# Four more idle transposes at the start of a fused threshold-attention and max-of-three feed-forward kernel, with a new written order

## The chip, the cores and the metric

The kernel runs on one core of one Trainium2 chip, in one launch. The metric is the device time of that launch in microseconds; smaller is better. The engines are called PE (matrix multiply; its weight loads are PEld), DVE (vector), ACT (scalar), POOL (GpSimd) and SP (the queue that issues most DMAs).

## The reference

Eight batches, eight heads, 576 positions of 64 dimensions. An attention keeps, in each row of scores, only the entries within tau = 0.02 of the row's maximum; its output, heads put side by side, is the input of a feed-forward step that takes the largest of three products.

```python
scores = scale * np.matmul(q, k.transpose(0, 1, 3, 2))
thresh = np.max(scores, axis=-1, keepdims=True) - tau
scores = np.where(scores >= thresh, scores, -1000000000.0)
scores = scores - np.max(scores, axis=-1, keepdims=True)
attn = np.exp(scores)
attn = attn / (np.sum(attn, axis=-1, keepdims=True) + 1e-09)
out = np.matmul(attn, v)
...
h = np.maximum(np.maximum(x @ w1, x @ w2), x @ w3)
return (h @ w_out).astype(np.float32)
```

q, k, v and the weights are float32; x is 4608 x 512, each of w1, w2, w3 is 512 x 768 and w_out 768 x 512.

## The kernel before

The heads of a batch are worked in two groups of four, called quads. For each quad and each half r (two heads), q and k are loaded (`load`), turned by PE with the help of an identity matrix into a PSUM bank (`transposed`, letter T) and copied out by ACT or DVE (letters a, A for q, c, C for k); POOL makes a second copy of q with its halves exchanged (`swapped`, q). Scores come in half tiles of 128 rows by 576 columns (`scores`, letter S): 288 of them, numbered in the order of the table TILES. One half tile is two pairs of float32 matmuls and fills one of four PSUM banks; the digit behind the letter S, T or F names the bank, and a bank can be filled again when its last reader is done.

A half tile then passes through DVE's maximum (m), ACT's exponent or threshold pass (e), and a second pass that makes the numerators and their sum (n on ACT, or k, a compare-multiply, on DVE). Which way it goes is a digit in the table MASKED: 1 and 3 take the second pass on DVE, 0 and 2 on ACT; 2 and 3 let ACT read the scores from PSUM, so that the bank is held until ACT has passed over it, while with 0 and 1 DVE's maximum frees it. A threshold (th) is made by DVE (s) or POOL (d). A reciprocal (r, DVE) and the normalization (p, POOL) follow, then a DMA that transposes the normalized tile P into ptq (t, on SP). The product of P and v (O, and its second half D, PE) is copied to xt by ACT (x) or DVE (w).

The feed-forward step of a batch begins when its xt is complete: F and B are the two halves of one unit on PE (`ph`, or `po` for the last product), h, H, v copy or combine the results, u, U copy the output to ob, o stores it. The first and the last batch are split in two parts, so that their feed-forward work can begin earlier.

Nothing is scheduled by a program at run time. The string ORDER is the written order: its letters are issued one after the other, each puts its instructions at the end of its engine's queue, and `_Ordered` ties each engine to that order. Capital letters among the copies choose DVE or ACT as said above. Each engine goes through its own queue in that order and waits where its operands or its bank are not ready.

Two groups of PE instructions compute nothing that is used: WARM transposes of the identity matrix at the very start, before the first q lands, and some more ahead of the second half of the first quad's q and k, inside `transposed`.

Of the kernel before, what the change touches and what calls it, by code (L numbers as in the profile page):

```python
# [47 lines left out]
ORDER = """
lllllllllllT2lT0lagqqcT3T2aS1CqqgS3ymgS0emS2ylnmS1emgemT3eS0AeT2kgS3nqmT1CqAnT2rkS1eqmCS0nqmepS2meS3prrmeS1p
tmnS0pS3snkptemeS2prmnzmtemepekpeS3lnS0ylrbyS1nlmtnpmnprremptebS3peS0mpnS1mS2znrmS0eptmnlpS3pemmdlrekS0S1ems  # L50
klT3nAnO20perewdDgpxtmnnT3S0prectpemS2mtS3npreqS0mT1pAptT3S1plqenmbnO02CdrkgmpDlxewzS3emlS0pF2meksBrF3HtS1Bd
S2nntqmetepvelnF0BS1mqS3egvzRnppmnT2nS0pmAdmrpS1peempeS2S1mgknpmegtrtF3BkHS0temS2pmetS1npS3mT2rszneF0mcnnyBs
rS1epsvnO32S0pemDpwsmpewS1nF3S0smrzBrqS1nstmF2vBsT3S0ppemHentnAS1psF2mlT3zyBqrgcvseS3F0nemgS2plpelnmepS3mtyB
ellqrmetqvnpS2sprdmO13fpsS0nDweS1mtewzkmnerS2S0F3dsnpS1mBpmeteepkF0mdtT2BnlulllneRnF1kAstS3pBHnmvF2epyRS0Btm
ppeS1S3vqtnmdS2F0pS1lpmndeT3empBCF2emslnlT3aT1kHdqeBctRvS0yF3S1pptnmnmprdpBF2qS0S1vmenBmltedS3S0HF1epmnrqT2B
mpseanS3veF2T0T1sCapkmBS0etvetyS1rS3ppmmkS0npeetmsO21S3neDxrtpmpnmqS0kS3smpkxS2rmemttpdS1eF0mlpesS3mrS2neBS1
keqnpduT3mlelmpS2O10sklelmCnekRsDwwldS3pteS1pmF2temqS0ntpnpssBeqS3mF1mhF0BBkF2RpS3veseBpvpT0S1ndmepS3HrdnmF2
typamnS0S1esmpnBmrF3vtpesF0S1BBpmvqnrT2enhsS1plS3ecdmnmF0nF2BBnrsptvyS1rveF3etneS0eymF2BS1tmkF0BhBS3ppmqtvlp
veO21edS0rkDmdnlmsnT0eppyxwkeF3loaS2qlT1BnpmesCnRS0HnpmS2seS1mF3mnsS0BeF2ptttpF1pmBBvelqS3lvnhS0snS2F1srrpmm
dF3metpdeBprBvpS2pvnnS0tmosetpS1eerF3ptemT2mAkBpS2UF1nmnnrS0ekqS3eedmmeS2eBptpmuekstlnS3elS0O12rxkmmsrkpDoS3  # L60
pS1rmppemT0oxdeS2N3lpncT1mBqS0nndF2yjtAkqqemT3cnRBdS1edHpF0S3mnepBemS2F1dvBnS3pnemF0tpeS2ntvlmRF1mpyBtdBhkvS
2emedT0F3appT1kttlCpBsS2vF0lpiS1S3mleBmnS2RehtdS1meF0mpnS3dmS2F1pssBtepemmBpnqS3vrnqF2T0dBvnS1mpeApS3rmhmedt
O02knrpleS1dseptnwpDmS0ennwT1lqrF3pmS2BF0pctmrvlqpS1nBemeS3vmdnF2etpeS1BmdtF0pS3BdkrhtmT2vS1ddpS3mekeamnlF0d
pdnRS2nmqF1peBlBepevlHF3nntqS2ppmS0BeF1T2BmvtrCpnS0dvtmS3S2ddpemmtrS1kentF0pS3nT2mBelprmnlpAtT1uS3pcS2eslmqO
01esktemDerwpeS2wS0qnmF1pnmdtnrkS3peS2spmoeBrnmptekS3F0puF2mBertkS1phBssmeS0yF3vnT1mndBllyS2AedyF0edmS1pnBrv
ptF2eS3permBtdpnHF1mlF0pervBdnBdyvetnS3F2HqS1mlnBlpmlS0dF3vpeeT1nlmBlF2kCS0RevBpnS1mpS3hsmpS0eF2smqnBmsnS1pr
veT0plS3maS2tekqO01emddDndmnpweywT3F2lncS0drqmBpF1eeS3yevdT0mBpadlS2HnF3qF0sntrmpBteBqvnsF1tpS2rnvT3pemBS0pt
CrHS2npS3mteF1rmF0dnBeBmyvpeS2lS1lvnpT3lmdeF0ptetsrmpnS2kopS1eBtsmnrmapS2elpS1mnrF3edpmUtS2emqT1neBpkteN0tcu
roS2kBpnS1jmdS3smmpelS0deT1rT2qpmcaS3esmO10nDkS3S2rpexwdmT1nmeanF0rdkleF3BpyS2nteS1sHpBpF0pemmS2rtvsmpqqnBtn
F1evdS3mBhS2repntpmS0mS1F3S2mtnpsrdsBF0S1senBvmdvF3F2etpBnnmqBF1dpHeT0evRBF3cS2vlyedmsBHF0eS1nBeS2tpmnnF3vpp  # L70
S1mrBpenO20tmdF1nvS3wBeskermkS2DelpenhsppqF3mpT1wenyBRS2vdmS0anmnS1mpeF3lS2mpnBqdS0ptF1F2spvimekeBrT3oldhpBv
S0mCeS1tenF3S2lmT0rBpamqS1yS0npS2rnvmmtdpF3eS0ekperBekdtmS1nteteF2pmskS0lmlptmkrBulsesT0ltS3prceS1unnqplmkdO
02lDemS1wqpppRpsS3eeS0mxpmF2lptS1msBS0ntnmS3HmeeymrF1T2dsBF0npS3pnaveesplrpeBtnF2S1BmpnvF0dmHqS3tBlnT2mvksF1
tS3BeCtmF0tF2snvBT3RsBF1eHvS0mepBpeS2atF3dvS0emneBF1nhmnS2nrqesBpO03nmpvwpeS2mnryokpS1DxosT2F0mpS3eecdpF1mtn
BS2qBS3servqphS0T1rmeF2maT3yBmnkS1pvdCmF0S3npBF1edtT2vpettBmF0akS2qheqdBrrsmpnevpS1nntF3pmS2qmBpS0vqmdeS1S2R
nF3T0pmpepCpttmsBS2S0nuF1mmeeksreS3eS0tBemtO32kspnDdrmpywkN3sduweS0onpBsneF1F2nreBjmS0psBnpHpmF3S1tvrpS0pmte
BF2remS1ptBvsF0eS3mBeodnshF2mS1tevBF0F3mBvS2nrF1nnklBmdhBesF2ppvveS0srppS3nreBymF1mS0S3nmemdtBeiphF2F0vdeBBt
vppS3F1nnkeS2mmdehBF0nrrdvnS3epBF2vppF1ntnmrtBthpS0esprsF3BnepeBnmnS2vS0ptpS1vemmmF3dkrS2mBtrS1eeumdO20deDne
O31wS2pDpwepnmnF0xwtkkS1prBS3pemrF1npusF2F0tmeBnpF3drBHpvtBepBnprF1tF2hBF3BvptpF0tvtF1BovhBBO32DvvO01xDxxF2x
uF0F3F2BohF1BF3BBuvovF2F0BoBF1hvvF3BF0hBBvvF2uF0N1BojUoi  # L80
"""


# [728 lines left out]
```

## Time and profile before

| what | value |
|---|---|
| median of the three runs | 443.31 us (441.85 to 444.83) |
| the profiled execution's own time | 444.28 us |
| its span in the trace | 442.5 us |
| mean granted PE clock | 0.983 |
| PE / DVE / ACT / POOL busy | 95% / 88% / 91% / 74% of the span |
| share of the last chain of waits by engine | PE 73%, DVE 7%, ACT 7%, POOL 4%, DMA 3% |
| DMA traffic | 87.98 MB, mean 199 GB/s |

The span is from the first to the last instruction of the trace; 1.8 us of the execution lie outside it. Busy matmuls have modelled ends, so a PE that is shown busy can still lose short times between two matmuls. The granted clock is 1 at full speed and 0.5 at half speed. Idle time in brackets behind a row is the engine's idle time before it, and what ended it.

### The profile page before, as it was taken

To read this page: it belongs to the slowest core of one execution; us is meant where nothing else is said; L and a number is where in the kernel's file an instruction comes from. 1 tells how busy PE (TensorE), PEld (TensorE's weight loads), DVE (VectorE), ACT (ScalarE), POOL (GpSimd) and SP (SyncE) were. 2 spreads that over 40 slices of the span, in tenths; PEclk is the share of its full clock that TensorE was granted. 3 is DMA by queue.
4 is the path that set the end of the run, shared out by engine and by line. 5 is a ranking of instruction groups with operands and counts; after the bars stand their busy time and mean duration, and the time that the engine had idled before them with its cause. 6 is when DMAs were issued, how large, how long until landed. Compare 5 with 4: busy or idle time off the path is not lost.

```text
span 442.5 us, 14396 instructions
## 1 busy us (share of the span) xinstructions
PE 422.4 (95%) x5355; PEld 313.3 (71%) x5355; DVE 389.6 (88%) x1112; ACT 401.9 (91%) x826; POOL 325.7 (74%) x495
## 2 busy tenths in 40 slices
PE   7868888999999999999999999999999999999995
PEld 5445646776687877778678876877778777886862
DVE  2989999999999999999999999999999888988522
ACT  2999999999999999999999999999999999899531
POOL 3698989898689678898788887867796775584400
PEclk8969999999999999999999999999999999999999
DMA  9999999999999999999999999999899757767911
GB/s 259 315 217 195 223 273 226 256 203 221 240 170 221 236 238 238 174 179 236 215 203 208 190 204 227 208 191 281 170 199 189 161 103 173 167 93 111 193 73 73
DMA packets 211590, 87.98 MB, mean 199 GB/s; under 512 B 186944, under 2 KB 199744, under 8 KB 211520
## 3 DMA queue, kind: packets, MB, share of 16 engines
q1 hardware_dynamic: 210704, 86.40, 96.2%
q8 instruction: 42, 0.69, 0.6%
q10 hardware_dynamic: 816, 0.66, 0.6%
q14 instruction: 28, 0.23, 0.2%
HBM read 35.13 MB, written 9.44 MB: 101 GB/s over the span
## 4 chain that ended last, share of the span: by engine, by line
PE 73%; DVE 7%; ACT 7%; POOL 4%; issue 4%; DMA 3%; POOLq 0%; SPq 0%; DVEq 0%
PE sc L100 27%; PE ph L100 24%; PE po L100 10%; PE o L100 8%; ACT z L100 6%; DVE z L100 4%; PE tp L100 3%; POOL P L100 3%; DMA ptq<-P 2%; DMA qm<-in_q_dram 1%; DVE hm L100 1%; POOL qs L100 1%; ACT ob L100 1%; DVE hT L100 1%; POOL w L100 0%
## 5 line engine op out<-in xcount | busy, mean ns | idle before, releaser
L100 POOL TENSOR_SCALAR P<-z,rs 128x576 bf16<-128x576 f32 x250 | 193.3, 784 | 43.3 <-DVE rs L100 15.7
L100 DVE TENSOR_SCALAR_CACHE_REDUCE z<-sc 128x576 f32<-128x576 f32 x250 | 182.9, 750 | 14.2 <-PE sc L100 10.3
L100 PE MATMUL sc<-kt,qs 64*128 64x256 f32 (+2 forms) x640 | 185.2, 421 | 7.0 <-ACT z L100 3.9
L100 PE MATMUL sc<-kt,qt 64*128 64x320 f32 (+2 forms) x640 | 186.2, 431 | 1.2 <-ACT obr L100 0.4
L100 PE MATMUL ph<-xt,w 64*128 64x288 bf16 (+2 forms) x2304 | 174.9, 283 | 0.7 <-DVE xt L100 0.3
L100 PEld LDWEIGHTS <-w 64*128 64x128 bf16 x2304 | 129.1, 94 | 31.3 <-issue 2.6
L100 ACT ACTIVATE z<-z 128x576 f32<-128x576 f32 x189 | 127.5, 680 | 0.6
L100 ACT ACTIVATE z<-z,th 128x576 f32<-128x576 f32 x162 | 120.4, 766 | 2.1 <-DVE th L100 1.3
L100 PEld LDWEIGHTS sc<-kt,qs 64*128 64x128 f32 (+1 forms) x640 | 92.7, 180 | 26.0 <-ACT z L100 6.3
L100 PEld LDWEIGHTS sc<-kt,qt 64*128 64x128 f32 (+1 forms) x640 | 92.7, 181 | 14.3 <-ACT z L100 2.9
L100 POOL COPY qs<-qt 64x640 f32<-64x640 f32 (+1 forms) x62 | 44.9, 723 | 16.6 <-ACT qt L100 8.8
L100 PE MATMUL po<-wo,hT 64*128 64x512 bf16 (+2 forms) x456 | 54.2, 354 | 0.5 <-DVE hT L100 0.4
L100 DVE SCALAR_TENSOR_TENSOR z<-z 128x576 f32<-128x576 f32 x61 | 50.5, 828 | 0.4 <-ACT z L100 0.3
L100 DVE TENSOR_TENSOR hm<-ph,hm 128x576 bf16<-128x576 f32 (+2 forms) x48 | 36.0, 751 | 14.5 <-PE ph L100 12.4
L100 PE MATMUL o<-ptq,vb 128*64 128x512 bf16 (+4 forms) x720 | 44.6, 277 | 1.3 <-DMA ptq<-P 0.7
L100 POOL TENSOR_SCALAR th<-nm 128x1 f32<-128x1 f32 x99 | 29.2, 295 | 20.0 <-DVE rs L100 4.9
L100 PEld LDWEIGHTS <-vb 128*64 128x64 bf16 (+1 forms) x720 | 26.0, 109 | 22.6 <-issue 12.1
L100 PEld LDWEIGHTS <-hT 64*128 64x128 bf16 (+1 forms) x456 | 29.2, 94 | 17.2 <-issue 1.7
L100 ACT ACTIVATE z<-z,nm 128x576 f32<-128x576 f32 x54 | 40.7, 767 | 0.0
L100 DVE TENSOR_TENSOR hT<-ph,hm 128x576 bf16<-128x576 f32 (+2 forms) x48 | 36.1, 753 | 2.2 <-PE ph L100 0.7
L100 ACT ACTIVATION_READ_ACCUMULATOR z<-z 128x1 f32 x189 | 37.2, 197 | 0.0
L100 POOL TENSOR_SCALAR P<-stage,rs 128x576 bf16<-128x576 f32 x38 | 29.0, 769 | 8.0 <-DVE rs L100 4.0
(55 smaller groups left out, 410.9 us busy)
## 6 DMA issues: line engine op xcount, KB each, us to landing
vm<-in_v_dram SPq DMA_DIRECT2D x32, 256.0 KB, 4.0
qm<-in_q_dram SPq DMA_DIRECT2D x15, 512.0 KB, 5.7
km<-in_k_dram SPq DMA_DIRECT2D x15, 512.0 KB, 5.5
out_dram<-ob SPq DMA_DIRECT2D x14, 512.0 KB, 4.4
ptq<-P SPq DMA_TRANSPOSE x144, 4.3
v<-in_v_dram SPq DMA_DIRECT2D x16, 96.0 KB, 3.8
hT<-in_moe_w_dram SPq DMA_DIRECT2D x3, 512.0 KB, 8.8
stage<-in_moe_w_out_dram SPq DMA_DIRECT2D x3, 512.0 KB, 6.0
```

Source lines behind the costliest of these rows:

```text
L100: ins = fn(*a, **kw)
```

## The change

The constant WARM goes from 13 to 14, and the idle transposes ahead of the second half of the first quad's q from 5 to 8; those ahead of k stay at one. The three tables are replaced. TILES is the same for the first 14 entries, exchanges entries 15 and 16, and differs throughout from the 46th on. MASKED is the same for the first two lines (144 half tiles) and differs in the other two: the digits 0, 1, 2, 3 occurred 193, 61, 27 and 7 times and now 189, 65, 27 and 7 times. ORDER has the same letters in nearly the same places for about eight lines of thirty, and another order from there on. These letters occur a different number of times:

| letters | before | after |
|---|---|---|
| n / k (second pass on ACT / DVE) | 220 / 68 | 216 / 72 |
| a / A (copy of q on ACT / DVE) | 20 / 12 | 14 / 18 |
| c / C (copy of k on DVE / ACT) | 16 / 16 | 13 / 19 |
| h / H (copy of ph on ACT / DVE) | 26 / 22 | 27 / 21 |
| u / U (copy to ob on ACT / DVE) | 15 / 3 | 11 / 7 |
| x / w (copy to xt on ACT / DVE) | 15 / 25 | 16 / 24 |
| s / d (threshold on DVE / POOL) | 94 / 99 | 94 / 95 |

```diff
-WARM = 13
+WARM = 14
...
 ORDER = """
-lllllllllllT2lT0lagqqcT3T2aS1CqqgS3ymgS0emS2ylnmS1emgemT3eS0AeT2kgS3nqmT1CqAnT2rkS1eqmCS0nqmepS2meS3prrmeS1p
-tmnS0pS3snkptemeS2prmnzmtemepekpeS3lnS0ylrbyS1nlmtnpmnprremptebS3peS0mpnS1mS2znrmS0eptmnlpS3pemmdlrekS0S1ems
...
+lllllllllllT1lT0lagqqcT3T2aS1CqqgS3mgS0emS2yynmeS1emgmT3eS0AeT2kgS3nqmT1CqAnT2rklS1eqmCS0nqmepS2eprrmS3emS1p
+tmnS0pS3smnkpteeS2prmnzmtemepekpeS2lS0ylrbyS1nnlmtnpmnprremptebS3peS0mnS1mS2znrpmS0eptmmnlpS3pemdlreekS0S1ms
...
             if L["first"] and r:
-                for _ in range(5 if n == "q" else 1):
+                for _ in range(8 if n == "q" else 1):
                     tensor.transpose(ps[:, 0:128], identf, identf)
```

PE's queue at the start of the program, before (qm and km are the loaded q and k, tp the bank that takes the turned tile, identf the identity):

```order
L100 MATMUL warm<-identf 128x128 x13
L100 MATMUL tp<-identf,qm 128x64 x8
L100 MATMUL tp<-identf,q_120 128x64 x2
L100 MATMUL tp<-identf,km 128x64 x8
L100 MATMUL tp<-identf,k_121 128x64 x2
L100 MATMUL tp<-identf 128x128 x5
L100 MATMUL tp<-identf,qm 128x64 x8
```

PE's queue at the same place after the change:

```order
L100 MATMUL warm<-identf 128x128 x14
L100 MATMUL tp<-identf,qm 128x64 x8
L100 MATMUL tp<-identf,q_121 128x64 x2
L100 MATMUL tp<-identf,km 128x64 x8
L100 MATMUL tp<-identf,k_122 128x64 x2
L100 MATMUL tp<-identf 128x128 x8
L100 MATMUL tp<-identf,qm 128x64 x8
```

One warming transpose is added ahead of the first q, three idle ones ahead of the second piece of q; nothing else moves here.

PE's queue at the 16th to 20th half tile of scores, before (each sc number is one half tile; in brackets the engine whose semaphore is waited for):

```order
L100 MATMUL sc_402<-kt_289,qs_256 128x320 [waits Activation_49]
L100 MATMUL sc_402<-kt_289,qt_255 128x256
L100 MATMUL sc_410<-kt_166,qs_160 128x256
L100 MATMUL sc_410<-kt_166,qt_159 128x320
L100 MATMUL sc_420<-kt_166,qs_160 128x320
L100 MATMUL sc_420<-kt_166,qt_159 128x256
L100 MATMUL sc_453<-kt_166,qs_160 128x256 [waits Activation_49]
L100 MATMUL sc_453<-kt_166,qt_159 128x320
L100 MATMUL sc_458<-kt_166,qs_160 128x320 [waits Activation_49]
```

The same half tiles in PE's queue after the change:

```order
L100 MATMUL sc_406<-kt_292,qs_259 128x320 [waits Activation_49]
L100 MATMUL sc_406<-kt_292,qt_258 128x256
L100 MATMUL sc_413<-kt_167,qs_161 128x256
L100 MATMUL sc_413<-kt_167,qt_160 128x320
L100 MATMUL sc_423<-kt_167,qs_161 128x320
L100 MATMUL sc_423<-kt_167,qt_160 128x256
L100 MATMUL sc_457<-kt_167,qs_161 128x256
L100 MATMUL sc_457<-kt_167,qt_160 128x320
L100 MATMUL sc_462<-kt_167,qs_161 128x320 [waits Activation_49]
```

The 16th half tile (sc_402, now sc_406) takes the bank of the 15th instead of that of the 14th, so its wait is for ACT's pass over the 15th; the 19th (sc_453, now sc_457) takes the bank that has been left and has no wait of its own any more.

ACT's queue near the end of the last batch's scores, before (z and stage are half tiles of scores in SBUF, ob the output):

```order
L100 ACTIVATE z<-z,nm 128x576
L100 ACTIVATE ob<-po 128x1024
L100 ACTIVATE z<-z,th 128x576
L100 ACTIVATE stage,sm<-stage 128x576
L100 ACTIVATE z<-z,th 128x576
L100 ACTIVATE z<-z,nm 128x576
L100 ACTIVATE z,sm<-z 128x576 x2
L100 ACTIVATE xt<-o 128x256
L100 ACTIVATE z<-sc,nm 128x576
L100 ACTIVATE z,sm<-z 128x576
L100 ACTIVATE ob<-po 128x1024
```

DVE's queue at that place after the change:

```order
L100 SCALAR_TENSOR_TENSOR z,sm<-z 128x576
L100 TENSOR_SCALAR z,nm<-sc 128x576
L100 TENSOR_SCALAR th<-nm 128x1
L100 RECIPROCAL rs<-sm 128x2 x2
L100 TENSOR_SCALAR z,nm<-sc 128x576 x2
L100 COPY ob<-po 128x1024
L100 RECIPROCAL rs<-sm 128x2
L100 SCALAR_TENSOR_TENSOR z,sm<-z 128x576
L100 TENSOR_TENSOR hm<-ph,hm 128x2x256
```

The last copy of two tiles of output, `ob<-po 128x1024`, was ACT's and is now DVE's.

More of the change, by code (lines that the diff above doesn't have):

```diff
@@ L26 @@
 011010100100100000000010001100000000000111102100100000101000000100001100
-000001001000110100000000100010000000000100100101000100000000000000110000
-100011011001000000100000001010000100001110000000010000001000000101001200
+000000101000110100010000100001000100000100000100000100000001100010000000
+000011010010000000000001011100100000001110001100001001000110000012100010
 """
 TILES = """
-065106157238442783620314785243875061513472860650738412860517432670315842
-153706824876320154368251704435708126526830174827610435510606158347278342
+065106157238447283620314785243875061513472860765830421817650432357816042
+762315804786502134175623084406235781126835704862107435065150618732423748
 """
-WARM = 13
+WARM = 14
 SLOTS = 4
@@ L48 @@
 ORDER = """
-lllllllllllT2lT0lagqqcT3T2aS1CqqgS3ymgS0emS2ylnmS1emgemT3eS0AeT2kgS3nqmT1CqAnT2rkS1eqmCS0nqmepS2meS3prrmeS1p
-tmnS0pS3snkptemeS2prmnzmtemepekpeS3lnS0ylrbyS1nlmtnpmnprremptebS3peS0mpnS1mS2znrmS0eptmnlpS3pemmdlrekS0S1ems
-klT3nAnO20perewdDgpxtmnnT3S0prectpemS2mtS3npreqS0mT1pAptT3S1plqenmbnO02CdrkgmpDlxewzS3emlS0pF2meksBrF3HtS1Bd
-S2nntqmetepvelnF0BS1mqS3egvzRnppmnT2nS0pmAdmrpS1peempeS2S1mgknpmegtrtF3BkHS0temS2pmetS1npS3mT2rszneF0mcnnyBs
-rS1epsvnO32S0pemDpwsmpewS1nF3S0smrzBrqS1nstmF2vBsT3S0ppemHentnAS1psF2mlT3zyBqrgcvseS3F0nemgS2plpelnmepS3mtyB
@@ L54 @@
[L54 to L78, printed above, removed]
@@ L79 @@
-O31wS2pDpwepnmnF0xwtkkS1prBS3pemrF1npusF2F0tmeBnpF3drBHpvtBepBnprF1tF2hBF3BvptpF0tvtF1BovhBBO32DvvO01xDxxF2x
-uF0F3F2BohF1BF3BBuvovF2F0BoBF1hvvF3BF0hBBvvF2uF0N1BojUoi
+lllllllllllT1lT0lagqqcT3T2aS1CqqgS3mgS0emS2yynmeS1emgmT3eS0AeT2kgS3nqmT1CqAnT2rklS1eqmCS0nqmepS2eprrmS3emS1p
+tmnS0pS3smnkpteeS2prmnzmtemepekpeS2lS0ylrbyS1nnlmtpnpmnrremptebS3peS0mnS1mS2znrpmS0eptmmnlpS3pemdlreekS0S1ms
+kT3nAnO20lpeerwdDgpxtmnnT3S0eprectpmS2mtS3nprqS0mT1epAptT3S1plqenmbnO20CdrmpDlkxewzS3eegmlS0pF2mksBrF3HtS1Bd
+S2nntqmeteepvlnF0BS1mqS3egvzRnppmT2nS0pmAndmrpS1peempeS2S1mgknpmegtretF3BkHS0tmS2pmetS1npS3mT2rsneF0zmsnyBcr
@@ new lines @@
+S1enpsvnO32S0peemDpwsmpwS1nF3S0smrzBrqS1nstmF2vBsT3S0ppemHenteAS1psF2mlT3zyBqrgcvsnS3F0nemgS2plpelnmepS3mtyB
+ellqrmetqvnpS2sprdmO13fpsS0nDweS1mtewzkmnerS2S0F3dsnpS1mBpmeteepkF2mdtT0BnlulllneRnF1kAstS3pBHnmvF0epyRS2Btm
+ppeS1S3vqtnmdS2F0pS1lpmneT3edCmpBF2emslnlT3aT1kHdqeBctRvS0ypF3S1ptnpmnmrdpBF2qS0S1vmenBmtedS3S0HepmnrqF1T2Bm
+pseanS3velF2T0sT1CapkmBS0etvetS1rS3ppmmkmS0npnO21eetS3seDxrpmpnmqS0kytS3smpkxS2rmettpdS1emF0pesS3mmrS2nelBS1
+nkmeqlduT3pmlpS2skeemCnO10kRsDwwldtS3pS1pmmtepeeF0S2qspdS3BmnmF1F2eneBBqhrkrF0S3pvpsBvT2S1snempndeapHterpllm
@@ new lines @@
+S3eF0mnS2dmS1myBqF3rF2nptS1vlsBsnBT0rmvpeS1ppnhncmS3mF2enntsrtF0BByevpF3rS1vemnppS2mF0eydBtS1thF2kBdBeS3tqmr
+vevnlpO01S2DpnlmexkesemT2pwadF3eplS0kdT1tmBCqRHeS2dmpS0onS1nF3lmS2nmBelynnF0F1tpdtmqspBBevvphS3S2rS0nsseemF1
+reF3ppmBntpBmrsdS0pveevS2nmmS1F3mlpertpT0BAypkepqS1UmnkF2tS0edS3entornS1mmBmtpeeueS3nS1ptkksrmmpO20ltnsrpDlk
+S1rpS3mmxS2epxepT0mqcdnN1eT3AkdnBF2S0jS3meT1deBeqqcRF0S1pHBS2mtF3mBdnppS1monennpvdlrstS2vF0meeF3mBnherBkpevS
+2lF1T0mappkslT3BrtvCnS2F0mpqS3S1detS2enBptmlmshpS3eS1prdmppmneF0lrlS2dF3ntBmmseBevsS2F1tpT0psBtrvymnAtS3hS2p
@@ new lines @@
+demnmO01S2kwenenpDS3ermT0nrwF2qlmtspncqpqrS1pedBF3mplevetS0plBS1mdeF2S0vpndBmmdorkhF3S1T2tBmS0eepS1ndatvdmtF
+3pktndmRF2S0plemnpBdvBF1HS0mS3enpmrpnBeF2eT0CdqevBnlS3S1vepS0S2qptmmenmtkrsF3nS0edT1pmtlAemBT2srS1puqeS0pncm
+nO32mekrtDweS0weqS1F2F3psmnpmnkplsS0eRkyepmByS1ekBmpsS0ypundmF2hS1RptemplBS0ndF3vdpmlT1BS2AdnmpevlF0S1BF2S3n
+rlmBF1emdeehF0kpeBvnS3veemBsF2S1hrtS0ntplqBlnpF3mmnT1vBqsRtkyS0pF2tteCevS1omppBnS3S0hF2ptldpndmmBsenmS3pT1ye
+aensvmeRS0etmpolS2skO31pDemT0wqwF2S3ctpdemBqF1ieS0T3pBvmS2tF0ndndaeF3hkymRdBqnvBF2pevsepS1lT0tBmpCrHpeS3ntS1
@@ new lines @@
+mS0nmdF2F3mBBS0perntnpevvpsnS1S2F3ltmrdepmepS0mBS2sT1kdmelUnF0tdS3nnpqmrS2ApnpT1BsemtS3RemnlN2CpS1kesBsppeer
+qUlmeS0mmS3T1jT2tS0mdnasceltpO13menslqDypS0wknrxpS1mpmlyF3dT2BldS0eAspntHnnrS1pmtF2merpF3BqeBsS0vnenrvyF1S2B
+enpS3mS0spptpmmmsS2heeF1rS3BpS0mF2nmF3mvteeBqtBF0eT1vHnkBF2S3dnsBrCnpF1vdemlS0BevqpykeF3mS2hrBprnmvF0eqtndts
+S1prmleBO32nspDpvpeF1S0nwekS3wsBmnepdtS2hmF0T1mdpBS2AF3vS1erBF0etndmS2nmrnpeS1vBnF3mpsnT2ylpRpdCoeHmBpS0dS2e
+vS1emmF3T0mBvS2asetpnnS0telpepqmmntrS1F3tpS2S0BmskeodmprtlknF1UeprmpqS2sT3eptcpmqsnBS0tS2mekudnS3O01Dkerpnmx
@@ new lines @@
+lexqrmpslS2dmpS3S1tF0mpleennermlS2BddF3mHnS1tpBrT0F2snmAS1eBevF0vpnptnqS3BmdlterHemtF2nslpS1tmBF0T3BpvsdCvyr
+F1nedeS3rpltpeF2T0meBBS3tAHvmpF0F1qtqBpS2vnBS3pF0mS2mneBkerkhelO13tqnesmevsxklrpDS2nS1xF0T3pBmtmF1eCepkdS3S2
+vBnrmpS0eS3phtmT2nF1mT0amnkpdBrqersvF3pS2BCF1S0mnT2BsevF3ompdrepqpS0thAmBdvS1peF2mtS0npBnmvS3S1S0deqrmpF2imT
+3nBnptsreCpmqS3UmnseS0ekmtrodeF1petS2tmkepeBS3kO02psmtrDwN3ndpuexerpS0meF1S2BeF0mBBnjF2hnS1kyskvdeptBS0mmrF3
+ptvdpS1nrpmBF0S2BnHnvF1epF3mBF0rveBBS2lykhF3vepS1mBnF0ddmS2F1venBS3mRtdHepmBnvS2depmS0oF3F1ptBmeBS0vehS3tnpn
@@ L81 @@
+knperlmsF2pF1mssBprvBppF3S0tvmeekBhnrteF2tS1F0BpmvsBenedS1nvmkrS3mpS2F0S1npetemrBmypeS2tO31umyspnDwwepO20xDe
+skerpkS1pmF2S3oS1snrntextprpBpmnmF3F1BF0epUBnhprtBkdepF3F2ttvnprBtpBvhvF1pF3tBvBHoF0F2BBO13vDxvO20wDF3wwF1F2
+F0oBHUuF1BBF2F3BhvoF0BvBiF1vF2BvF3BhvBvF2F1ouN0Bujooi
 """
```

## The prediction

> **What bounds the kernel now.** I read the page's share of busy time first, then busy time by stretches of the span.
>
> ```profile
> PE 422.4 (95%) x5355; PEld 313.3 (71%) x5355; DVE 389.6 (88%) x1112; ACT 401.9 (91%) x826; POOL 325.7 (74%) x495
> ...
> 20.00:30.00 10.00, 6.38 (x34) 3.52 (x30) 8.95 (x27) 10.00 (x24) 10.00 (x13) 0.75 0.92 217
> 40.00:60.00 20.00, 17.09 (x192) 11.08 (x188) 19.93 (x56) 19.33 (x44) 18.80 (x26) 1.00 1.08 208
> ...
> 100.00:150.00 50.00, 49.88 (x636) 36.46 (x636) 48.66 (x147) 49.23 (x101) 39.58 (x60) 1.00 1.12 214
> ...
> 350.00:400.00 50.00, 50.00 (x666) 38.89 (x665) 43.73 (x128) 47.97 (x99) 34.88 (x56) 1.00 0.66 132
> ```
>
> The columns behind each stretch are PE, weight loads, DVE, ACT, POOL, then the granted clock. There are two regimes. In the first 60 us the elementwise engines are full (ACT 10.00 of 10.00 us, DVE 19.93 of 20) and PE waits for them. From 100 to 400 us PE is full and ACT and DVE lie 1 to 13% below it. A microsecond won early counts only if it brings the start of the PE-bound stage forward; one won later counts only if PE gets it.
>
> Early on PE also loses its clock. These stretches follow the steps of the granted clock, 3.41 us long, from 1.09 us on (columns: PE busy, granted clock).
>
> ```profile
> 1.09:4.50 3.41, 3.04 (x13) 1.00 0.81 215
> 4.50:7.92 3.42, 2.05 (x33) 1.00 1.09 343
> 7.92:11.33 3.41, 3.41 (x25) 0.50 1.12 313
> 11.33:14.74 3.41, 2.73 (x28) 1.00 1.09 353
> ...
> 21.57:24.98 3.41, 1.42 (x9) 1.00 1.01 182
> 24.98:28.40 3.42, 2.35 (x10) 0.50 1.00 205
> 28.40:31.81 3.41, 2.85 (x12) 0.50 1.17 310
> 31.81:35.22 3.41, 3.41 (x17) 0.50 1.17 185
> 35.22:38.64 3.42, 2.51 (x37) 1.00 0.85 211
> ```
>
> Each row's clock was settled by the row above it. After 2.05 and 1.42 us of work the next window runs at half; after 2.51 and more it stays full. A half-clock window with 2.35 or 2.85 us of work is followed by another; only 3.41 of 3.41 releases it. In this trace, then, the clock falls below a limit between 2.05 and 2.51 us of work and returns at one between 2.85 and 3.41. The Trainium skill (TensorE: Matmul & The Clock Gate, "Why this matters for your kernels") asks for no idle gap over about 3 us between bursts. The trace disagrees: the 2.05 us window has no idle time over 0.71 us (next fence), and the clock fell.
>
> **The change, part by part.**
>
> *Idle transposes at the start.* The PE and DVE rows around the first lost window:
>
> ```profile
> 1.34 3.04 PE L100 MATMUL warm<-identf 128*128 128x128 f32 x13 [1.34 <-POOL identf masks.py:199]
> 4.81 0.46 PE L100 MATMUL tp<-identf,qm 64*128 64x64 f32 x8 [0.43 <-DMA qm<-in_q_dram]
> ...
> 6.15 0.76 PE L100 MATMUL tp<-identf 128*128 128x128 f32 x5
> 7.62 0.50 PE L100 MATMUL tp<-identf,qm 64*128 64x64 f32 x8 [0.71 <-DMA qm<-in_q_dram]
> ...
> 8.94 0.74 PE L100 MATMUL sc<-kt,qs 64*128 64x256 f32 x1
> ...
> 18.71 0.53 PE L100 MATMUL sc<-kt,qs 64*128 64x320 f32 x1
> 18.72 0.70 PE L100 MATMUL sc<-kt,qt 64*128 64x256 f32 x2
> 19.09 0.43 PE L100 MATMUL sc<-kt,qs 64*128 64x320 f32 x1
> ...
> 10.36 0.76 DVE L100 TENSOR_SCALAR_CACHE_REDUCE z<-sc 128x576 f32<-128x576 f32 x1 [1.15 <-PE sc L100]
> ```
>
> An idle transpose takes at most 3.04 / 13 = 0.23 us. The fourteenth fits into the 0.43 us before the first q lands. Three more before the second piece of q take at most 0.70 of the 0.71 us in which PE waits for that piece: no cost. If the data came at once they would delay the chain by up to 0.70 us. The window 4.50 to 7.92 goes from 2.05 to some 2.75 us of work, above the 2.51 that kept the clock. Then 7.92 to 11.33 runs at full speed. The first half tile of scores runs from 8.94 until DVE can start at 10.36, 1.42 us; at full clock one takes 19.09 + 0.43 - 18.71 = 0.81. That is 0.6, and the eight transposes of k ahead of it, at half speed too, give about 0.3 more; the second half tile, on which DVE waited again, brings it to about **-1.0 us**. The bounds are 0 (the clock falls anyway) and -1.4 (all of those 1.42 us). What is behind is ACT and DVE in a full queue, so the shift is kept until PE takes over.
>
> *The bank of the sixteenth half tile.* Its scores go to bank 2 instead of bank 3 (the second pair of rows in the section on the change). That falls into the second slow stretch:
>
> ```profile
> 26.05 0.90 PE L100 MATMUL sc<-kt,qs 64*128 64x320 f32 x1 [2.41 <-ACT z L100]
> ...
> 29.96 0.79 PE L100 MATMUL sc<-kt,qs 64*128 64x256 f32 x1 [0.56 <-ACT z L100]
> ...
> 23.94 2.69 ACT L100 ACTIVATE z<-sc,nm 128x576 f32<-128x576 f32 x4
> ...
> DVE z L100 <- PE sc L100: 1.5, 5, 0.6
> ```
>
> Before, these scores wait at 26.05 for the third of the four ACT passes that start at 23.94; with bank 2 they wait for the fourth, 2.69 / 4 = 0.67 later. In return the nineteenth half tile no longer waits at 29.96: its bank 3 has been free since. PE then works without a gap from about 26.7, the window 28.40 to 31.81 fills, and full clock should come back one window earlier, at 31.81. The last row is DVE's wait for scores from 26.5 to 36.2 us, 1.5 in all, most of it in the last slow window. I take 1.1 of it as won and 0.6 as lost to the later start: **-0.5 us**, between +0.7 (no window won) and -1.5.
>
> *Engine choices and masks.* Counted in the two tables: four more half tiles are masked on DVE (68 to 72), so ACT loses four second exponent passes and DVE gains four compare-multiplies. Six copies of q and, net, four of ob go from ACT to DVE, three of k the other way; one hm and one xt go to ACT, and POOL gets four th fewer. Nothing changes engine before the 73rd half tile, and little before the 145th.
>
> ```profile
> L100 ACT ACTIVATE z<-z 128x576 f32<-128x576 f32 x189 | 127.5, 680 | 0.6
> L100 DVE SCALAR_TENSOR_TENSOR z<-z 128x576 f32<-128x576 f32 x61 | 50.5, 828 | 0.4 <-ACT z L100 0.3
> L100 ACT ACTIVATE qt<-tp 128x640 f32<-128x640 f32 (+1 forms) x20 | 12.8, 642 | 5.0 <-PE tp L100 5.0
> L100 DVE TENSOR_SCALAR qt<-tp 128x640 f32<-128x640 f32 (+1 forms) x12 | 9.0, 752 | 0.0
> L100 ACT ACTIVATE ob<-po 128x1024 f32<-128x1024 f32 (+1 forms) x15 | 14.0, 932 | 5.3 <-PE po L100 4.6 <-PE sc L100 0.5
> L100 DVE COPY ob<-po 128x1024 f32<-128x1024 f32 (+1 forms) x3 | 3.1, 1045 | 2.0 <-PE po L100 2.0
> L100 DVE COPY kt<-tp 128x512 f32<-128x512 f32 (+1 forms) x16 | 11.7, 730 | 0.0
> ```
>
> ACT: -4 x 0.68 - 6 x 0.64 - 4 x 0.93 + 3 x about 0.65 + two copies of about 0.6 = about -7. DVE: 4 x 0.83 + 6 x 0.75 + 4 x 1.05 - 3 x 0.73 - two of about 0.7 = about +8. DVE has the room: from 350 to 400 it is idle 6.3 us of 50.
>
> *The new written order.* PE's own work is the same but for four transposes. What can be won behind 100 us is PE's waiting. By the two rows above, PE shows 0.12 idle of 50 us and none, so the end near to the rows is about -1 over 300 us. Matmul ends are modelled, and short waits can hide in them; the other end is ACT's -7, had ACT set the pace throughout. I take **-2.0**, near PE's row. On the bad side the added DVE work stays covered (0) or delays PE (rival below).
>
> Sum against the profiled execution: 444.28 - 1.0 - 0.5 - 2.0 = 440.8. That execution lies 0.97 above the median of 443.31. If every run of before lost the first window, the median falls by 3.5 to 439.8; if the median run did not, by 2.5 to 440.8. I take **440.3**.
>
> **The rivals.**
>
> *The transposes don't hold the clock.* The window 4.50 to 7.92 holds transposes alone, and the clock fell behind it; perhaps they don't count at all. Against it: 1.09 to 4.50 holds only the 13 warming transposes, and the clock stayed at 1.00 behind it. Without the first term the time is 440.3 + 1.0 = 441.3. Chance 0.15. The Trainium skill (TensorE: Matmul & The Clock Gate, "Part 4: PE-mode transpose") says that transposes don't count as PE work in the same way and don't bring full clock. By that rule the change would not do what it says here; the first row speaks against it.
>
> *ACT set the pace after all.* PE's 49.88 of 50 would then hide many short waits for ACT, which was at 49.23. All of ACT's 7 us less come through: 443.3 - 1.5 - 7 = about 435. For it: ACT's share is as high as that of a bound engine. Against it: from 350 to 400 ACT has 2 us of room and PE none. Chance 0.16.
>
> *Products come too early.* Each product of P and v waits for the last transpose through the DMA, which lands late:
>
> ```profile
> ptq<-P SPq DMA_TRANSPOSE x144, 4.3
> ...
> 338.04 4.35 DMA ptq<-P
> ...
> PE o L100 <- DMA ptq<-P: 0.7, 2, 0.4
> ```
>
> PE waited little for it so far, because PE work written ahead hides the 4.3 us. In the new order the products of the fifth batch have less of it written between the last transpose and themselves: by counts of score pairs, feed-forward halves and products about 2 and 4 us where there were 9 and 7. If this cover is gone, each of the twelve products behind the first batches can wait up to 4.3 us. It decides in favour of slower once such waits come to over 5.9 us: 4.4, one per cent, and the 1.5 won early. With four products waiting 1.9 us each: 443.3 - 1.5 + 7.6 = 449.4. Chance 0.10.
>
> **How the numbers follow.** The forecast has 0.59, with an own range of 437.5 to 443.5. One per cent, about what a measurement of this kernel can tell from no change (the three runs span 3 us), is 4.4: the marks are 438.9 and 447.7. Faster: 0.16 from ACT's rival and 0.10 from the low end of the forecast, 0.26. Slower: 0.10. Within: 0.64. The range runs from 436 (into ACT's rival) to 446 (towards the late products) and leaves out less than 0.2.
>
> **What would show it.** Right: the windows up to 11 us all at 1.00, DVE's first maximum near 9.3, a second slow stretch of two windows rather than three, ACT near 395 and DVE near 397 us busy, PE's stretches full from about 60 us on. Wrong: half clock at 7.92 in spite of about 2.7 us of work ahead of it; ACT waiting between 28 and 33 us because the sixteenth half tile came late; PE waits for ptq of several us; or a new slow window, which would cost PE 1.7 us each.

## The result, and the profile after

Twenty runs of each kernel: 440.73 us (439.84 to 441.89) after the change, 443.44 us (440.52 to 446.2) before. The ratio is 0.9945 with a 95% interval of 0.9929 to 0.9962, so the change wins 0.55%, 2.4 us by the ratio; the two medians lie 2.7 us apart. The profiled execution of the changed kernel took 440.52 us, 3.76 less than the profiled one of before; its span is 438.7 us and its mean granted clock 0.992.

The page's line of busy time, the changed kernel:

```profile
PE 418.6 (95%) x5357; PEld 315.5 (72%) x5359; DVE 396.3 (90%) x1126; ACT 393.7 (90%) x813; POOL 324.4 (74%) x491
```

ACT has 8.2 us less than before, DVE 6.7 more; PE, whose work is the same but for four transposes, is busy 3.8 us less. The stretches of the span that were shown of before (PE, weight loads, DVE, ACT, POOL, granted clock):

```profile
20.00:30.00 10.00, 5.63 (x29) 3.62 (x28) 9.25 (x26) 10.00 (x24) 10.00 (x12) 0.80 1.19 237
...
100.00:150.00 50.00, 49.24 (x645) 36.95 (x642) 47.48 (x142) 48.62 (x99) 39.24 (x61) 1.00 1.07 216
...
350.00:400.00 50.00, 50.00 (x651) 39.24 (x649) 45.67 (x128) 43.67 (x89) 34.05 (x54) 1.00 0.76 150
```

From 20 to 30 us the granted clock is 0.80 where it was 0.75. From 100 to 150 us PE is even a little less full than before (49.24 against 49.88). What ACT was relieved of shows from 350 to 400 us: 43.67 where there were 47.97. The two kernels stand at different points of their work there, so these rows don't say where the time went. That is read further below from the start of the same work in both traces.

PE in the steps of the granted clock, which in this run begin at 2.14 us (columns: PE busy, granted clock):

```profile
2.14:5.56 3.42, 3.42 (x27) 1.00 1.06 310
5.56:8.97 3.41, 3.36 (x41) 1.00 1.15 314
8.97:12.38 3.41, 2.68 (x28) 1.00 1.05 360
...
22.62:26.04 3.42, 1.05 (x8) 1.00 1.16 206
26.04:29.45 3.41, 2.73 (x12) 0.50 0.99 328
29.45:32.86 3.41, 3.41 (x16) 0.50 1.27 172
```

Up to 12 us every row shows 1.00. That is not a measurement everywhere: the trace's record of the clock begins at 5.56 us here and at 4.50 us in the trace of before, and ahead of its first record a row shows 1.00. The idle transposes tell the speed there. In both traces they start mostly 0.21 us apart ahead of that point and 0.11 us apart behind it, so PE began at about half speed and came to full speed there. From 5.56 to 12 us no window is lost any more. The second slow stretch, from 26.04 to 32.86, has two windows where before had three. PE and DVE at the start of the program and PE at the 16th half tile, from the timeline (start, length, work, and in brackets the idle time before and what ended it):

```profile
5.84 1.09 PE L100 MATMUL tp<-identf 128*128 128x128 f32 x8
6.87 0.46 PE L100 MATMUL tp<-identf,qm 64*128 64x64 f32 x8
...
24.99 0.53 PE L100 MATMUL sc<-kt,qs 64*128 64x320 f32 x1 [3.04 <-ACT z L100]
...
28.90 0.90 PE L100 MATMUL sc<-kt,qs 64*128 64x320 f32 x1 [0.68 <-ACT z L100]
...
8.67 0.76 DVE L100 TENSOR_SCALAR_CACHE_REDUCE z<-sc 128x576 f32<-128x576 f32 x1 [0.24 <-PE sc L100]
```

The second piece of q starts at 6.87 without a wait, 0.75 us earlier than in the trace of before: here its data had landed by then. DVE's first maximum starts at 8.67 instead of 10.36. The 16th half tile waits 3.04 us for ACT, 0.63 longer than before, as its bank is freed one ACT pass later; the 19th waits no more, the 20th 0.68 us at 28.90.

### The profile page after: what moved, and what is told of

It reads as the page before. It is cut to its first block, busy times and chain, and to the rows that moved or that the text cites. A ratio compares the mean times of both kernels' runs of the same rounds, so it can differ in the third digit from the quotient of the medians.

```text
span 438.7 us, 14399 instructions
## 1 busy us (share of the span) xinstructions
PE 418.6 (95%) x5357; PEld 315.5 (72%) x5359; DVE 396.3 (90%) x1126; ACT 393.7 (90%) x813; POOL 324.4 (74%) x491
## 4 chain that ended last, share of the span: by engine, by line
PE 76%; ACT 9%; DVE 6%; issue 3%; DMA 3%; POOL 1%; SPq 1%; DVEq 0%; POOLq 0%; ACTq 0%
PE ph L100 28%; PE sc L100 26%; PE po L100 10%; ACT z L100 8%; PE o L100 8%; PE tp L100 4%; DVE z L100 4%; DMA qm<-in_q_dram 2%; DMA ptq<-P 1%; DVE hm L100 1%; POOL P L100 1%; PE warm L100 1%; SPq L100 1%; DVE hT L100 0%; DVE kt L100 0%
## 5 line engine op out<-in xcount | busy, mean ns | idle before, releaser
L100 PE MATMUL sc<-kt,qs 64*128 64x320 f32 (+2 forms) x640 | 181.5, 416 | 7.9 <-ACT z L100 5.0
L100 PE MATMUL sc<-kt,qt 64*128 64x256 f32 (+2 forms) x640 | 183.0, 427 | 0.9 <-ACT z L100 0.4
L100 ACT ACTIVATE z<-z 128x576 f32<-128x576 f32 x186 | 125.5, 679 | 0.3
L100 ACT ACTIVATE z<-z,th 128x576 f32<-128x576 f32 x159 | 118.6, 767 | 1.6 <-DVE th L100 1.0
L100 PEld LDWEIGHTS sc<-kt,qt 64*128 64x128 f32 (+1 forms) x640 | 91.6, 178 | 15.1 <-DVE z L100 2.5
L100 DVE SCALAR_TENSOR_TENSOR z<-z 128x576 f32<-128x576 f32 x64 | 51.5, 807 | 0.1
L100 PE MATMUL o<-ptq,vb 128*64 128x512 bf16 (+4 forms) x720 | 43.5, 276 | 1.2 <-DMA ptq<-P 0.7
L100 ACT ACTIVATE z<-z,nm 128x576 f32<-128x576 f32 x57 | 43.1, 768 | 0.0
L100 PEld LDWEIGHTS <-hT 64*128 64x128 bf16 (+1 forms) x456 | 31.1, 94 | 15.7 <-issue 2.4
```

Source lines behind the costliest of these rows:

```text
L100: ins = fn(*a, **kw)
```

## The experiments

Each kernel is compared with runs of the kernel before beside it on the same chip (their median is 442.68, 443.62 or 443.13 us); a ratio below 1 is faster than before, and the brackets hold its 95% interval. "Worse than the change by" is the difference of two such ratios, times 443.

### The idle transposes alone, and the rest without them

The first kernel is before with the two numbers of the change:

```diff
-WARM = 13
+WARM = 14
...
-                for _ in range(5 if n == "q" else 1):
+                for _ in range(8 if n == "q" else 1):
```

> The kernel before with 14 and 8 idle transposes and nothing else changed. Theory A (the forecast: idle transposes 1.0, bank 0.5, late order 2.0 us): 443.4 - 1.0 = 442.4 us, clock full from 4.5 to 11.3 us, spread over the runs hardly smaller. Theory B (all of the gain is the clock at the start; the reordering is neutral): 440.7 us, and the runs of before's wide spread (440.5 to 446.2) shrink to about 2 us. Theory C (all of it is the new order): 443.4 us.

Measured: 442.48 us against 442.68, ratio 0.9993 [0.9976, 1.001]. The second kernel is the changed one with the two numbers put back to 13 and 5:

> The kernel after with 13 and 5 idle transposes, new order, masks and banks kept. A: 441.7 us. B: 443.4 us with a wide spread. C: 440.7 us. By A and B the window behind the first transposes runs at half clock in the profile whenever the gaps fall into one window.

Measured: 440.07 us, ratio 0.9946 [0.9931, 0.9962]. So the transposes alone win nothing that can be measured, and without them the change wins all it did. A reason is to be seen in the windows of the second kernel's trace:

```profile
4.39:7.81 3.42, 2.63 (x38) 1.00 1.10 344
7.81:11.22 3.41, 3.23 (x28) 1.00 1.11 309
```

With five idle transposes the window at 4.39 holds 2.63 us of work, and the clock stays. The row of PE's timeline that makes the difference is this one:

```profile
6.99 0.46 PE L100 MATMUL tp<-identf,qm 64*128 64x64 f32 x8 [0.42 <-DMA qm<-in_q_dram]
```

The second piece of q is waited for 0.42 us, not 0.71, and it begins 0.63 us earlier than in the trace of before. Besides, the windows have another place in each trace: they begin at 1.09 us and every 3.41 after it in the trace of before, at 0.98 in this one, 2.14 after the change, 0.63 in the first experiment's. So whether the early window is lost depends on when the data land and on where the windows lie.

How many windows a run has at half can be read from the mean granted clock that each run lists. One window at half speed takes 3.41 x 0.5 / 442 = 0.004 from it; by the traces, 0.992 stands for two windows (after the change), 0.988 for three (the first experiment) and 0.983 for four (before). Four would leave 0.985 at most, so the runs with 0.986 have three and some half speed at the very end, as the trace of before has it from 441.41 us on. The 59 runs of before beside all these experiments:

```
mean granted clock   runs   windows at half   median us   against the median of its group
0.994 to 0.996        22     one               442.93      -0.02
0.990 to 0.992        24     two               443.35      +0.19
0.986 to 0.988        12     three             442.76      -0.09
0.983                  1     four              445.01      +1.39
```

A clock as low as that of the profiled run, 0.983, came once in 59. One, two or three windows make no difference that shows. But this clock tells how many windows a run lost and not which, and it leaves out the half speed ahead of the first record, so it doesn't say how often the early window was lost.

The traces say more. DVE's first maximum starts at 8.46 to 8.95 us in four of the five traces with five idle transposes, and at 10.36 in the fifth, which is before's. In the nine traces with eight idle transposes it starts at 8.67 to 9.46 us in eight, and at 10.93 in one, in which PE came to full speed only at 10.37 us (the experiment with q and k put back, below). So the early loss was one trace in five, and eight transposes bring the first maximum no earlier on the whole. They do hold the clock in the case that the prediction had in mind. In the trace of the experiment on the masks (below) the windows begin at 4.46 us, nearly as before, and the second piece of q is waited for 0.76 us; with eight idle transposes ahead of it the next window stays at full clock, and DVE's first maximum starts at 9.35:

```profile
4.46:7.87 3.41, 2.43 (x37) 1.00 1.08 339
7.87:11.28 3.41, 3.31 (x36) 1.00 1.10 274
```

### The bank of the 16th half tile

The changed kernel with one digit put back, as the kernel before had it:

```diff
-tmnS0pS3smnkpteeS2prmnzmtemepekpeS2lS0ylrbyS1nnlmtpnp
+tmnS0pS3smnkpteeS2prmnzmtemepekpeS3lS0ylrbyS1nnlmtpnp
```

> The kernel after with the scores of the 16th half tile in bank 3 again, all else kept. A: they start 0.67 us earlier, the 19th wait again, the second slow stretch lasts three windows, 0.5 us slower: 441.2 us. B and C: the digit is worth nothing, 440.7 us.

Measured: 441.1 us (439.44 to 443.29), ratio 0.9962 [0.9943, 0.9981]. PE's windows and waits are those of before again:

```profile
23.80:27.21 3.41, 2.34 (x10) 0.50 1.00 210
27.21:30.63 3.42, 2.86 (x12) 0.50 1.13 309
30.63:34.04 3.41, 3.41 (x17) 0.50 1.14 193
```

Three windows at half instead of two. In the runs it is as in the trace: eight of the twelve have a clock of 0.986 to 0.988, while all twenty runs of the changed kernel have 0.990 or more. So within the new order the bank saves a window in most runs. Between the kernel before and the changed one there is less to save: 46 of the 59 runs of before have one window at half or two, as all twenty of the changed kernel have. In time the digit is worth 0.9962 - 0.9945 = 0.0017 of 443, about 0.75 us, but the two intervals overlap; the size is not settled.

The next kernel goes further: the half tiles from the 16th to the 26th take their banks in the order in which the banks come free, and all later digits are exchanged to fit (0 with 1, 2 with 3).

```diff
-peS2lS0ylrbyS1nnlmtpnpmnrremptebS3peS0mnS1mS2znrpmS0ep
+peS1lS0ylrbyS3nnlmtpnpmnrremptebS2peS1mnS0mS3znrpmS1ep
```

> The kernel after with the banks of the 16th half tile and all later ones renamed so that each takes the bank that ACT frees first; the order of work on every engine is kept. If the wait of PE at 22 to 25 us and the half clock behind it still cost the elementwise engines time (DVE waits 1.3 us for scores from 24 to 36 us), the 16th half tile starts about 23.0 instead of 25.0 us, PE is evenly spread over the windows, DVE's wait goes, and the time falls by about 1 us to 439.7. If ACT alone sets the pace there, PE's idle time shrinks and the time stays at 440.7.

Measured: 440.0 us, ratio 0.9944 [0.9931, 0.9957], the same as the changed kernel's. Its windows and its wait at this place:

```profile
22.22:25.63 3.41, 2.26 (x17) 1.00 1.21 228
25.63:29.04 3.41, 0.94 (x7) 1.00 0.90 295
29.04:32.45 3.41, 3.41 (x16) 0.50 1.24 206
```

One slow window is left of two, and in this trace PE is 0.76 us ahead of the changed kernel at 130 us and still some 0.9 ahead at 429; in the medians this can't be told from nothing.

### The head alone and the tail alone

The changed kernel's order and table of half tiles up to the 86th half tile, with the idle transposes, and before's order and masks behind it; and the other way round, before's head with 13 and 5, and everything of the change behind the 86th half tile.

The first line of each table that differs from before, in the first and in the second of them:

```diff
-065106157238442783620314785243875061513472860650738412860517432670315842
+065106157238447283620314785243875061513472860650738412860517432670315842
...
-WARM = 13
+WARM = 14
...
-lllllllllllT2lT0lagqqcT3T2aS1CqqgS3ymgS0emS2ylnmS1emgemT3eS0AeT2kgS3nqmT1CqAnT2rkS1eqmCS0nqmepS2meS3prrmeS1p
+lllllllllllT1lT0lagqqcT3T2aS1CqqgS3mgS0emS2yynmeS1emgmT3eS0AeT2kgS3nqmT1CqAnT2rklS1eqmCS0nqmepS2eprrmS3emS1p
```

```diff
-000001001000110100000000100010000000000100100101000100000000000000110000
+000000101000110100010000100001000100000100000100000100000001100010000000
...
-065106157238442783620314785243875061513472860650738412860517432670315842
+065106157238442783620314785243875061513472860765830421817650432357816042
...
-keqnpduT3mlelmpS2O10sklelmCnekRsDwwldS3pteS1pmF2temqS0ntpnpssBeqS3mF1mhF0BBkF2RpS3veseBpvpT0S1ndmepS3HrdnmF2
+nkmeqlduT3pmlpS2skeemCnO10kRsDwwldtS3pS1pmmtepeeF0S2qspdS3BmnmF1F2eneBBqhrkrF0S3pvpsBvT2S1snempndeapHterpllm
```

> The kernel after up to the 86th half tile (there both orders have issued the same work into the same banks), the kernel before behind it; 14 and 8 idle transposes. Differences against before of the same chip. If the early edits (transposes, bank, shuffles) carry the gain: -2.5 us. If it lies behind the 86th half tile: between 0 and -0.7 us. The traces so far (gain of PE's finished work against the run with idle transposes alone: 1.3 us at 36 us, 0.3 at 244 us, 2.9 at 420 us) speak for the second.

> The kernel before up to the 86th half tile with its 13 and 5 idle transposes, the kernel after behind it. If the gain is in the late order: -2 to -2.5 us against before. If it is early: 0 to -0.5 us.

Measured: the new head 443.12 us against 443.62, ratio 0.9997 [0.997, 1.0024]; the new tail 440.85, ratio 0.9941 [0.992, 0.9962]. The gain lies behind the 86th half tile. The early part, bank and transposes included, is worth nothing that these runs can tell; the interval leaves it at most 1.3 us.

### The engine choices alone, and the order without them

The changed kernel with 13 of its late engine choices put back: six copies of q to ACT, three of k to DVE, four of ob to ACT. And before with 13 of its own late letters exchanged in the same numbers. One of the places of each:

```diff
-3nBnptsreCpmqS3UmnseS0ek
+3nBnptsrecpmqS3umnseS0ek
...
-S0deT1rT2qpmcaS3esmO10nDk
+S0deT1rT2qpmCAS3esmO10nDk
```

> The kernel after with thirteen copies given back to the engines they had before (six q copies and four ob copies from DVE to ACT, three k copies from ACT to DVE, late in the program), same order and masks. ACT gets about 5.6 us more work, DVE about 6.5 less. If the relief of ACT carries the late gain: slower than the kernel after by 2 us or more (about 442.7). If the written order carries it and ACT is covered: 440.7, at most 0.5 more.

> The kernel before with the same thirteen copies given to the engines of after (six q and four ob copies from ACT to DVE, three k copies from DVE to ACT), order and masks of before. If the relief of ACT carries the late gain: -2 us against before. If it needs the order that goes with it: 0, or slower, because copies now stand in DVE's queue at places that were chosen for ACT's.

Measured: the order without the choices 445.87 us, ratio 1.0061 [1.0036, 1.0086], 5.1 us worse than the change; the choices without the order 448.93, ratio 1.0113 [1.0082, 1.0143]. The second relieves ACT of 3.6 us (its page has 398.3 busy, before's 401.9) and is 5.0 us slower than before. The first result alone would speak for ACT's relief as the cause. The second shows that relief is not enough: at these places, in the old order, it does harm. The three longest of PE's waits between 200 and 425 us in the second kernel, by the view of waits (total, times, longest):

```profile
PE tp L100 <- DVE z L100: 1.0, 1, 1.0
PE o L100 <- DVE z L100: 0.6, 1, 0.6
PE ph L100 <- DVE qt L100: 0.5, 1, 0.5
```

In the trace of before PE waits in this stretch for ACT once (0.4 us) and for the DMA twice (0.7). Now the longest waits are for DVE, which got the copies: two for passes over z, one for a copy of q.

### Which choices

Two kernels put back a part each: the four copies of ob, and the nine of q and k.

```diff
-qUlmeS0mmS3T1jT2tS0mdnasc
+qulmeS0mmS3T1jT2tS0mdnasc
...
-tdS3nnpqmrS2ApnpT1BsemtS3
+tdS3nnpqmrS2apnpT1BsemtS3
```

> The kernel after with only the four ob copies given back to ACT. The thirteen copies together cost about 5 us against after. If each copy costs by its length (four of 0.93 us of the 5.6 us on ACT): about 3 us of the 5. If it is the order that breaks where one of them lands, most of the 5 us falls either here or with the q and k copies.

> The kernel after with the six q copies given back to ACT and the three k copies to DVE. By length: about 2 us slower than after. By place: most of the 5 us or next to none.

Measured: ob back 442.2 us against 443.13, ratio 0.998 [0.9966, 0.9993], 1.6 us worse than the change; q and k back 445.41, ratio 1.0045 [1.0029, 1.0061], 4.4 us worse (0.010 of 443). Both traces show where some of it goes. With ob back on ACT, PE and ACT from the timeline:

```profile
267.51 1.43 ACT L100 ACTIVATE stage<-stage,th 128x576 f32<-128x576 f32 x2
268.84 1.01 ACT L100 ACTIVATE ob<-po 128x1024 f32<-128x1024 f32 x1
...
269.90 0.43 PE L100 MATMUL sc<-kt,qs 64*64 64x256 f32 x2 [0.91 <-ACT ob L100]
```

In the changed kernel the same copy is DVE's, and PE's scores, which take the bank that it frees, come without a wait:

```profile
267.54 1.23 DVE L100 COPY ob<-po 128x1024 f32<-128x1024 f32 x1
...
268.98 0.43 PE L100 MATMUL sc<-kt,qs 64*64 64x256 f32 x2
```

The copy on DVE takes longer (1.23 against 1.01 us) and ends 1.1 us earlier, as it doesn't stand behind two threshold passes. At this place PE pays for the end of a copy, not for its length. The largest wait with q and k back has the same form, a copy of q behind a pass of z on ACT and a bank that PE needs:

```profile
340.33 0.77 ACT L100 ACTIVATE z<-z,nm 128x576 f32<-128x576 f32 x1
341.00 0.59 ACT L100 ACTIVATE qt<-tp 128x512 f32<-128x512 f32 x1
...
341.64 1.65 PE L100 MATMUL ph<-xt,w 64*128 64x288 bf16 x24 [0.86 <-ACT qt L100]
```

This wait is about a fifth of the 4.9 us that the profiled execution loses behind 244 us (the table further below); the rest has several places and was not followed to each.

### The masks

The changed kernel with four of its masked half tiles unmasked again, so that ACT makes their second pass; in the order their k becomes n, and an s, their threshold on DVE, is written behind their m:

```diff
-000000101000110100010000100001000100000100000100000100000001100010000000
-000011010010000000000001011100100000001110001100001001000110000012100010
+000000101000010100010000100001000100000100000000000100000001100010000000
+000011010010000000000000011100100000001110001000001001000110000012100010
```

> The kernel after with four late half tiles (the 157th, 190th, 240th and 262nd) unmasked: their second pass goes from DVE to ACT (0.68 to 0.88 us each) and DVE makes a threshold for each. If ACT's relief carries the late gain, 1 to 2.7 us slower than after (about 442 to 443.5); if ACT has cover there, within 0.5 us of it.

Measured: 446.37 us against 443.13, ratio 1.0071 [1.0057, 1.0084], 5.6 us worse than the change, more than the 2.5 us of work that ACT got (its page: 396.2 against 393.7). Almost all of it is lost at one place. The chain of waits there (start, length, what), and PE's timeline:

```profile
365.05 0.77 POOL P L100 x2
365.82 3.23 DMA ptq<-P
...
369.19 4.19 PE o L100 x36
```

```profile
366.65 0.40 PE L100 MATMUL o<-ptq,vb 64*64 64x512 bf16 x2 [0.89 <-DVE z L100]
369.19 4.19 PE L100 MATMUL o<-ptq,vb 64*64 64x512 bf16 x38 [2.13 <-DMA ptq<-P]
```

At the same work the changed kernel's chain holds PE alone:

```profile
364.05 0.43 PE sc L100 x4
364.48 2.51 PE o L100 x39
```

In the experiment the last tile for these products reaches POOL and the transposing DMA too late, and PE stands 0.89 and then 2.13 us. PE in the steps of the granted clock there (busy time, clock):

```profile
366.28:369.70 3.42, 0.92 (x10) 1.00 0.66 128
369.70:373.11 3.41, 3.41 (x30) 0.50 0.53 103
```

The window with the two waits holds 0.92 us of work, the next one runs at half, and the products take 4.19 us where they take 2.51. 0.89 + 2.13 + 1.68 = 4.7 of the 5.1 us that are lost between the same two points of PE's work.

### The exchanged banks without the idle transposes

The kernel with the exchanged banks, with 13 and 5 idle transposes in place of 14 and 8:

```diff
-WARM = 14
+WARM = 13
...
-                for _ in range(8 if n == "q" else 1):
+                for _ in range(5 if n == "q" else 1):
```

> The kernel after with the banks in the order in which ACT frees them and with 13 and 5 idle transposes. If the clock and PE's early wait are worth nothing in the median: the same ratio to before as the kernel after, 0.9945, so about 440.7. If the banks win what the trace showed early (0.9 us) and the idle transposes are worth nothing: 439.8.

Measured: 440.15 us against 443.13, ratio 0.9922 [0.9907, 0.9937]. It is the lowest ratio of all, but the kernel with the banks alone lies at 0.9944 [0.9931, 0.9957] against other runs of before, and the intervals overlap. It is not shown to beat the changed kernel.

### Where the time goes, step by step

Between two traces a loss can be placed: count PE's matmuls by the columns that they stream, their share of the array and their type, and note when each trace has started the same amount of this work. How many us each kernel lies behind the changed one, in one trace of each. The first column is the changed kernel's time; "idle only" is before with the idle transposes, the others are the experiments with ob, with q and k, and with four masks put back.

```
changed kernel at   idle only   ob back   q, k back   masks back
 59.1                 1.2         0.1        2.0         0.6
130.5                 0.9        -0.1        1.9         0.9
244.2                 0.3        -0.1        2.0         0.7
276.2                 1.2         0.9        2.7         1.3
307.4                 1.4         0.7        5.1         1.1
338.9                 1.4         1.0        6.7         1.3
354.7                 2.4         1.0        6.7         1.3
370.5                 2.2         1.2        6.9         6.4
428.7                 2.9         1.5        6.9         6.4
```

What differs at 59 us is in part the fortune of one run; with q and k back, DVE's first maximum came 2.26 us later than in the changed kernel's trace, and 2.0 stand in the table. What comes behind 244 us is the change: before's order loses 2.6 there, in one step of 0.9 near 271 us and several of about 0.3. The step of 0.9 is in the chain of waits of the profile of before:

```profile
269.32 0.67 ACT ob L100
...
270.25 0.77 ACT z L100 x2
271.01 0.50 ACT obr L100
...
271.55 0.76 PE sc L100 x6
```

Before, PE's scores wait at 271.55 for the copy obr on ACT, which stands behind ob and two passes; the view of waits shows 0.4 us of this as idle time of PE. It is the same place at which the copy put back cost 0.9. In the changed kernel's chain there is PE alone at this place (the same view):

```profile
268.40 0.65 PE po L100 x12
269.05 1.20 PE sc L100 x14
270.25 0.77 PE tp L100 x20
```

The steps of 0.3 have no wait beside them that the trace shows, and what makes them was not settled. Nor does any run part the new order of the half tiles (TILES) from the new order of the letters behind the 86th half tile.

## Why the prediction was right

The time, 440.3 us, the sign and the range held, and the bound of one per cent too. The steps that it was summed from did not hold alike, and that the sum came within half a microsecond is in part luck: a first step that is worth nothing and a third that was too small made up for each other.

**The idle transposes, -1.0.** This step failed. The mechanism exists: in the one trace with the data as late and the windows nearly where before had them, eight transposes kept the clock. But the transposes alone gave 0.9993 [0.9976, 1.001], and the early window was lost in one of five traces with five transposes, the one that the step was read from. The prediction had left open how the median run stood to this window, with 440.8 for the case that it doesn't lose it, and took a value between the two cases. The second case is the one that fits. Two readings in this step were wrong besides. The row from 1.09 to 4.50 lies ahead of the clock's first record: PE ran at half speed there and came to full speed at its end. And the 0.23 us of an idle transpose was taken from that row; at full speed they start 0.11 us apart, so three more bring the window from 2.05 to about 2.4 us of work, not to 2.75 (2.43 was seen with eight).

The rival that transposes don't hold the clock gave 441.3 for the same sum without this term. Its result came near, but not its mechanism. In the first experiment 30 transposes alone fill the window ahead of the clock's first record at 7.45 us. The idle ones among them start 0.21 us apart, at half speed, and behind that window PE is at full speed (its two windows, then the idle ones in PE's timeline):

```profile
4.04:7.45 3.41, 3.41 (x30) 1.00 1.09 337
7.45:10.87 3.42, 3.32 (x36) 1.00 1.12 307
```

```profile
6.01 1.77 PE L100 MATMUL tp<-identf 128*128 128x128 f32 x8
```

The rule of the Trainium skill (TensorE: Matmul & The Clock Gate, "Part 4: PE-mode transpose") that transposes don't count as PE work is not borne out by this trace, in which transposes alone brought PE to full speed. The eight idle ones take 1.77 us ahead of the record here, and 1.09 behind the record in the changed kernel's trace.

**The bank of the 16th half tile, -0.5.** The mechanism was right: the wait grew by 0.63 (0.67 was said), the 19th half tile no longer waits, and two windows at half are left of three in the two profiles. Like the first step it was read from an unusual run, though: 13 of the 59 runs of before have three windows or more. The size, 0.75 us between the two ratios, agrees, and is not settled, since the head alone gave 0.9997 [0.997, 1.0024]. What the step took for granted, that a slow window there is paid for in the end, is not seen in the medians: runs of before with three windows at half are no slower than those with one.

**The engine choices and the new order, -2.0.** The tail alone measured 0.9941 [0.992, 0.9962], which is -2.6 us, and from -1.7 to -3.5 by the interval. The step lay between PE's idle time in the rows of before (about 1) and ACT's work (7), nearer to the first, and so does the result. It was a little small: PE's waits that the trace of before shows between 200 and 425 us come to 1.1 us, so more than half of what was won doesn't show as idle time. The account of ACT's and DVE's work was right within 1.3 us (393.7 and 396.3, foretold 395 and 397), but relief by itself was not the cause: with thirteen copies moved in the old order, ACT has 3.6 us less and the kernel loses 5.0. The prediction had no step for this, that the choices are worth something only at the places where the order leaves room for them.

**The rivals.** *ACT set the pace* would have given 435, with ACT's 7 us coming through. It fell: ACT lost 8.2 and the time 2.4. *Products come too early* did not come: PE's waits of the changed kernel between 200 and 425 us, as the trace shows them, are

```profile
PE sc L100 <- DVE hT L100: 0.2, 1, 0.2
PE po L100 <- DVE th L100: 0.2, 1, 0.2
```

and none of them is for ptq; over the whole span its waits for ptq come to 0.7 us, as before. But the mechanism is there: four masks fewer, and one of these waits comes, 2.13 us long, with the slow window behind it that the prediction priced at 1.7.

## What to carry to other kernels

Where PE is full and two elementwise engines are nearly so, ask of a copy when it ends on each engine and which bank PE gets by that, not how long it is: a longer copy on the engine that is free at that moment won 0.9 us, and relieving the busier engine at the wrong places lost 5. Engine choices, masks and written order are one plan; a part of it taken alone can be worth less than nothing. An event in one profiled run, here a slow window at the start, is a term of the sum only after other traces have shown how often it comes; the mean clock of a run tells how many windows were slow, not which.

## What the runs showed of the hardware that was not expected

The clock's windows have no fixed place against the program: their edges, followed back, lay at 0.63, 0.98, 1.09 and 2.14 us in four traces. PE begins at half speed. In all 14 traces the idle transposes start mostly 0.21 us apart ahead of the first record of the clock and, where any come behind it, 0.11 us apart; that record lies between 4.15 us (the new head) and 10.37 us (q and k back). Rows ahead of it show 1.00, and the mean granted clock doesn't count it.

A share of busy time in the window before does not settle the clock alone. In the 14 traces a window at full clock with 2.12 us of work or more was followed by full clock, and one with 1.43 or less by half. In between both were seen: half behind 2.05 (before), full behind 1.71 (the bank put back, at 433.39 us), 1.92 (the new head, at 51.93) and 2.09 (the changed kernel, at 19.21). So the lower limit that the prediction read from one trace does not hold in the others. At half clock 2.89 us of work brought the full clock back in the trace of the new tail (from 24.14 us on), and 2.86 did not with the bank put back.

By the mean clocks of the runs of before, three windows at half cost nothing that shows against one (12 and 22 runs); in the traces these windows lie in the first 40 us. One window at half in the stage that PE bounds cost the whole 1.7 us.
